# Group 0's low halves all on VectorE, and the first two groups' softmax of q by head on ScalarE

## The chip, the cores and the metric

The kernel runs on one NeuronCore of one Trainium2 chip, as one launch. The metric is the device time of the program in microseconds; lower is better. Three runs of the kernel before took 1586.83, 1587.82 and 1588.03 us; their median is 1587.82 us.

## The reference

A linear attention is followed by two gated feed-forward blocks. q, k and v have the shape (8, 8, 576, 64): batch, heads, positions, features of a head.

```python
q_s = softmax of q over its 64 features      # per position and head
k_s = softmax of k over its 576 positions    # per head and feature
kv  = k_s^T @ v                              # 64 x 64 per head
x   = q_s @ kv, heads side by side           # 4608 tokens x 512
xn  = x / sqrt(mean(x*x) + 1e-6) * rms_g
x   = (silu(xn @ w_gate) * (xn @ w_val)) @ w_out     # d_ff 1536
h   = max(x @ w1, x @ w2, x @ w3)                    # d_ff 768
out = h @ w2_out
```

The softmax of q takes away the maximum of each head first and adds 1e-9 to the sum that it divides by.

## The kernel before

The 4608 tokens are worked on in nine groups of 512 tokens (the ninth collects the last 64 positions of each batch). Each group's attention is made in four pairs of heads, p = 0 to 3; a pair's q is a tile of 128 tokens x 8 x 64 (four blocks of 128 tokens times two heads). While one group runs through the first feed-forward block, the attention of the next is made beside it; group 0's own attention comes first, in a prologue of staged calls (the table `stages`).

**A group's feed-forward** is twelve steps f (`iteration`), one for each 128 of the 1536 inner features. In each, TensorE computes pg (gate) and pv (value), 12 matmuls each, and adds the step before to four accumulators (`out1`), 12 more. Every product is made of three matmuls, on operands that are split in a high part, rounded by ScalarE (ACT), and a low part, the rest of a subtraction: hi*hi, hi*lo and lo*hi. So `hh` and `hl` are the two parts of the hidden values t, `wh` and `wl` those of the weights, `xh` and `xl` those of the input. t itself is tanh on ACT (L651), then two operations on VectorE (DVE): L652, which reads pg, and L663, which reads pv. pg has one bank of PSUM, so pg of a step can start when L652 of the step before has read it.

**The weights come as 64-bit words** and are made into floats on the chip, once, during group 0, one step f + 1 ahead of its use (class `Weights`). A step's weights are two halves h of 128 x 768. For each half, ACT scales the upper words (L144), DVE joins the words in three operations (L149, L150, L151, "the joins" below), ACT rounds the high part (L162) and a subtraction gives the low part (L168): half 0's on GpSimd (POOL), half 1's on DVE. The columns of pg lie in half 0. In group 0 up to step 10 the subtraction for `hl` (L670) is POOL's too, and in all other groups DVE's.

**The softmax of q** (`q_exp`, `q_divide`) takes for a pair: the maximum of each head on DVE (L281, qm), a subtraction on POOL (L282), exp on ACT in place (L283), the sum on DVE (L287, qs), an addition and a reciprocal on DVE (L288, L290) and the product on POOL (L291). After that TensorE transposes q (`transpose_q`). POOL also makes the low part of group 0's input (L389) and adds up squares (L379).

**Group 0's normalisation** is needed only at the first hidden value: pg and pv of steps 0 and 1 are made from the input that is not yet normalised (`raws`), and the result is multiplied by the scale z (L649, giving u_0, and L662). z comes from four sums (var, L410) by a chain of ten small operations on DVE (`token_rstd`, L421 to L426), a transpose on TensorE and a copy on ACT (`spread_rstd`).

A scheduler orders the instructions of each engine when the program is built, by its own estimate of each duration; each engine then works strictly in that order and waits at the first instruction whose inputs are not there. So a line that moves to another engine also moves other instructions. COMPACT is the set of groups 0 and 1, whose scale is computed in the small form.

Of the kernel before, what the change touches and what calls it, by code (L numbers as in the profile page):

```python
# [8 lines left out]
F32 = mybir.dt.float32  # L9
F32R = mybir.dt.float32r  # L10
I32 = mybir.dt.int32
AF = mybir.ActivationFunctionType
ALU = mybir.AluOpType
AX = mybir.AxisListType

P = 128
# [9 lines left out]
COMPACT = (0, 1)  # L26
# [18 lines left out]
def attention_moe_moe(ctx: ExitStack, tc: tile.TileContext, q, k, kt, v, w1, rms_g, w2, w2_out, out):  # L45
# [14 lines left out]
    nc = tc.nc  # L60
# [4 lines left out]
    two = ctx.enter_context(tc.tile_pool(name="two", bufs=2))  # L65
# [3 lines left out]
    def bank(tag, name):  # L69
        return ps.tile([P, N], F32, tag=tag, name=name)  # L70
# [39 lines left out]
    for i in range(2):  # L110
        t = one.tile([P, P], F32, tag=f"kv_raw{i}", name=f"kv_raw{i}")
# [6 lines left out]
    class Weights:  # L118
# [45 lines left out]
        def low(self, f, h):  # L164

            hi = wh[1, f].rearrange("p j n -> p (j n)")[:, h * HALF : (h + 1) * HALF]
            engine = nc.gpsimd if h == 0 else nc.vector
            engine.tensor_sub(self.half(1, f, h), self.y.pop((f, h)), hi.bitcast(F32))  # L168

    class Ahead:  # L170

# [82 lines left out]
    q_t, k_t, kT_t, v_t, kv8 = {}, {}, {}, {}, {}  # L254
    kmax, xraw, sacc, qrt, rstd = {}, {}, {}, {}, {}

    def load_pair(g, p):
# [14 lines left out]
        else:  # L272
            kv8[p] = []
            for i in range(2):
                t = two.tile([P, 4, P], F32, tag=("k", "v")[i], name=f"kv8_{p}_{i}")
                nc.sync.dma_start(t, kv_dram[p, :, 4 * i : 4 * i + 4, :])
                kv8[p].append(t)

    def q_exp(g, p):
        qm = two.tile([P, 24], F32, tag="qm", name=f"qm_{g}_{p}")[:, 0:8]  # L280
        nc.vector.tensor_reduce(qm, q_t[g, p], axis=AX.X, op=ALU.max)  # L281
        nc.gpsimd.tensor_sub(q_t[g, p], q_t[g, p], qm.unsqueeze(2).to_broadcast([P, 8, 64]))  # L282
        nc.scalar.activation(q_t[g, p], q_t[g, p], AF.Exp)  # L283

    def q_divide(g, p):
        qs = two.tile([P, 8], F32, tag="qs", name=f"qs_{g}_{p}")
        nc.vector.tensor_reduce(qs, q_t[g, p], axis=AX.X, op=ALU.add)  # L287
        nc.vector.tensor_scalar(qs, qs, EPS_SM, None, op0=ALU.add)  # L288
        qr = two.tile([P, 8], F32, tag="qr", name=f"qr_{g}_{p}")
        nc.vector.reciprocal(qr, qs)  # L290
        nc.gpsimd.tensor_mul(q_t[g, p], q_t[g, p], qr.unsqueeze(2).to_broadcast([P, 8, 64]))  # L291

    def k_max(g, p):
        if g == NB:
            return
        km = two.tile([P, 1], F32, tag="km", name=f"km_{g}_{p}")
        nc.vector.tensor_reduce(km, kT_t[g, p], axis=AX.X, op=ALU.max)
        kmax[g, p] = km

    def k_exp(g, p):  # L300
        if g == NB:
            return
        pb = pair_bank(g, p, "pb", "a1")
        nc.tensor.transpose(pb[:, 0:P], kmax[g, p].to_broadcast([P, P]), ident)
        nc.vector.tensor_sub(k_t[g, p], k_t[g, p], pb[:, 0:P].unsqueeze(1).to_broadcast([P, 5, P]))
        nc.scalar.activation(k_t[g, p], k_t[g, p], AF.Exp)
# [25 lines left out]
    def transpose_q(g, p):  # L332
        pt = pair_bank(g, p, "pt", "a1")
        for t in range(4):
            nc.tensor.transpose(
                pt[:, t * P : (t + 1) * P], q_t[g, p][:, 2 * t : 2 * t + 2, :].rearrange("p a d -> p (a d)"), ident
            )
        if g in WHOLE:
            if g == 0 and p > 0:
                if p == 1:  # L340
                    sqs["q"] = wpool.tile([P, 3, N], F32, tag="wl5", name="qrts")
                qrt[g, p] = sqs["q"][:, p - 1, :]
            else:
                qrt[g, p] = pair_tile(one, [P, N], F32, "qh", g, p)
            nc.scalar.copy(qrt[g, p], pt)
            return
        qh[g, p] = pair_tile(one, [P, N], F32R, "qh", g, p)
        ql[g, p] = pair_tile(one, [P, N], F32R, "ql", g, p)
        split(qh[g, p], ql[g, p], pt)
# [163 lines left out]
    acc, hh, hl = {}, {}, {}  # L513
# [90 lines left out]
    def iteration(g, nxt, f):  # L604
        ahead = g == 0 and f + 1 < NF1
        pair, odd = f // 2, f % 2

        if ahead:
            first.scale(f + 1, 0)
        if nxt is not None:  # L610
            if not odd and 1 <= pair <= 4:
                transpose_q(nxt, pair - 1)
                make_kv(nxt, pair - 1)
                if pair + 1 < 4:
                    load_pair(nxt, pair + 1)
            if odd and 1 <= pair <= 4:
                make_x(nxt, pair - 1)
            if pair < 4 and not odd:
                k_max(nxt, pair)
                q_exp(nxt, pair)  # L620
            if pair < 4 and odd:
                k_exp(nxt, pair)
                q_divide(nxt, pair)
            if f == 10 and nxt in COMPACT:
                token_rstd(nxt)
            elif f == 10:
                variance(nxt)
                newton_step(nxt, 0)
                newton_step(nxt, 1)
            if f == 11:  # L630
                if nxt not in COMPACT:
                    newton_step(nxt, 2)
                for p in range(4):
                    normalise(nxt, p)
        elif f == 1:
            load_raw(0)
        if ahead:
            first.join(f + 1, 0)
            first.scale(f + 1, 1)
        wkey = (1, f)  # L640
        raw = g == 0 and f < NRAW
        xhs = [(rawh[p] if raw else xh[g, p]) for p in range(4)]
        xls = [(rawl[p] if raw else xl[g, p]) for p in range(4)]
        pg = bank("G", f"pg_{g}_{f}")
        product_in(pg, wh[wkey], wl[wkey], 0, xhs, xls)
        t = two.tile([P, N], F32, tag="t", name=f"t_{g}_{f}")
        if raw:
            u = two.tile([P, N], F32, tag="y", name=f"u_{g}_{f}", bufs=3)
            nc.vector.tensor_mul(u, pg, rstd[0][1])  # L649
            pg = u  # L650
        nc.scalar.activation(t, pg, AF.Tanh, scale=0.5)  # L651
        nc.vector.scalar_tensor_tensor(t, t, 1.0, pg, op0=ALU.add, op1=ALU.mult)  # L652
        if ahead:
            first.high(f + 1, 0)
            first.join(f + 1, 1)
        pv = bank("V", f"pv_{g}_{f}")
        product_in(pv, wh[wkey], wl[wkey], 1, xhs, xls)
        if nxt is not None and f == 11:
            for p in range(4):
                split_x(nxt, p)  # L660
        if raw:
            nc.vector.tensor_mul(t, t, rstd[0][1])  # L662
        nc.vector.tensor_mul(t, t, pv)  # L663
        hh[g, f] = two.tile([P, N], F32R, tag="hh", name=f"hh_{g}_{f}")
        hl[g, f] = two.tile([P, N], F32R, tag="hl", name=f"hl_{g}_{f}")
        nc.scalar.copy(hh[g, f], t)  # L666
        if ahead:
            first.low(f + 1, 0)
            first.high(f + 1, 1)
        (nc.gpsimd if ahead else nc.vector).tensor_sub(hl[g, f], t, hh[g, f].bitcast(F32))  # L670
        if nxt is not None and f == 9 and nxt not in COMPACT:
            split_squares(nxt)
        if f > 0:
            out1(g, f - 1)
        elif g > 0:
            out1(g - 1, NF1 - 1)
        if nxt in COMPACT and f == 10:
            spread_rstd(nxt)
        if g > 0 and nxt is not None:
            if g == 1 and f == 0:  # L680
                second.load()
                second.load()
            second.advance(f)
            if g == NG - 2 and f == NF1 - 1:
                assert not second.steps
        if nxt is None:
            if 1 <= f <= 3:
                fetch(2)
            if f in (4, 5):
                for n in range(4 * f - 16, 4 * f - 12):  # L690
                    combine(0, n)
            if f >= 6:
                for which in {6: (B11,), 7: (T2,), 8: (T1,), 9: (T3,), 10: (B21, B22), 11: (T4,)}[f]:
                    split_operand(which)
            if f == 11:
                fetch_out(0)
        if ahead:
            first.low(f + 1, 1)
            first.load(f + 4)
        if g == 0 and f == NRAW - 1:  # L700
            for p in range(4):
                normalise(0, p)
                split_x(0, p)
# [100 lines left out]
    for pr in range(NPAIR):  # L804
        g = 2 * pr
        for u in range(UNITS):
            fp, j = divmod(u, 3)
            if j == 0:
                t = {
                    key: two.tile([P, N], F32, tag=tag, name=f"t2_{pr}_{fp}_{tag}")  # L810
                    for key, tag in (((0, 0), "q"), ((0, 1), "k"), ((1, 0), "v"), ((1, 1), "t"))
                }
# [23 lines left out]
    g = NG - 1  # L836
    for u in range(UNITS):
        fp, j = divmod(u, 3)
        pair = [bank(tag, f"p2_{g}_{u}_{tag}") for tag in (("G", "V"), ("a0", "a1"))[u % 2]]
        if j == 0:  # L840
            t = [two.tile([P, N], F32, tag=tag, name=f"t2_{g}_{fp}_{tag}") for tag in ("q", "k")]
# [76 lines left out]
```

## Time and profile before

| | |
|---|---|
| median of three runs | 1587.82 us |
| the profiled execution: its own time, and its span | 1587.12 us, 1585.3 us |
| PE busy | 1538.8 us (97% of the span) |
| DVE busy | 865.9 us (55%) |
| ACT busy | 529.3 us (33%) |
| POOL busy | 270.1 us (17%) |
| mean granted TensorE clock | 0.989 |

The span is what the rows lie in; about 1.8 us of the execution lie around it. The shares are means over stages of different kinds. In the page's picture of 40 slices of 40 us, PE is below nine tenths only in the first four, and DVE, which works at five or six tenths later on, is at nine tenths in the first three; POOL has three to five tenths there and two or less afterwards. A row of a timeline is start, duration, engine, line, operation, tiles and shape. A duration on DVE is the time from an instruction's start to its end, and it contains time in which the instruction could not get on.

### The profile page before, as it was taken

The page shows a single profiled execution, that of the slowest core. Times are in us where ns is not written, and L with a number is a line of the kernel's source. Part 1 is how long each engine was busy: PE and PEld are TensorE (multiplying, and loading weights), DVE is VectorE, ACT ScalarE, POOL GpSimd, SP SyncE. Part 2 cuts the span into 40 slices and gives each one's busy share as a digit, 9 for nine tenths or more (in the row PEclk, how much of TensorE's full clock was granted, in tenths as well). Part 3 has the DMA queues.
Part 4 walks back from the last instruction along what each step waited for, and adds up shares of the span by engine and source line. Part 5 has one row for each costly group of instructions (what it writes and reads, how often), then busy time and mean ns, then how long its engine had stood idle before and what let it go on. Part 6 is the DMA issues. An engine that isn't in the chain of part 4 may idle for free.

```text
span 1585.3 us, 18644 instructions
## 1 busy us (share of the span) xinstructions
PE 1538.8 (97%) x6974; PEld 1269.1 (80%) x6974; DVE 865.9 (55%) x1450; ACT 529.3 (33%) x919; POOL 270.1 (17%) x308
## 2 busy tenths in 40 slices
PE   5788999999999999999999999999999999999999
PEld 3566788888888888888888888888888888888887
DVE  6999654655655655656552243535645644634412
ACT  4553433433433444344332231322322322322221
POOL 4355222122120231221200100001001001001000
PEclk8899999999999999999999999999999999999999
DMA  7662143331340541434301013164544554444441
GB/s 258 238 226 84 61 138 106 104 119 53 126 133 24 164 139 62 152 115 139 100 22 53 14 47 127 53 226 163 187 175 164 183 177 164 161 173 165 134 153 47
DMA packets 92889, 203.33 MB, mean 128 GB/s; under 512 B 8448, under 2 KB 36096, under 8 KB 92800
## 3 DMA queue, kind: packets, MB, share of 16 engines
q1 hardware_dynamic: 82432, 183.27, 34.6%
q10 hardware_dynamic: 10368, 18.88, 3.2%
q8 instruction: 55, 0.90, 0.2%
q14 instruction: 34, 0.28, 0.1%
HBM read 161.48 MB, written 40.63 MB: 127 GB/s over the span
## 4 chain that ended last, share of the span: by engine, by line
PE 90%; DVE 5%; DMA 1%; issue 1%; POOL 1%; ACT 0%; SPq 0%; DVEq 0%; POOLq 0%; ACTq 0%
PE acc L482 9%; PE acc L481 9%; PE acc L483 9%; PE pg L475 6%; PE pg L477 6%; PE pg L476 6%; PE pv L477 6%; PE pv L476 6%; PE pv L475 6%; PE p_a L481 5%; PE p_a L483 5%; PE p_a L482 5%; PE p_G L481 2%; PE p_G L483 2%; PE p_G L482 2%; PE pk L315 2%
## 5 line engine op out<-in xcount | busy, mean ns | idle before, releaser
L652 DVE SCALAR_TENSOR_TENSOR t<-t,pg 128x512 f32<-128x512 f32 x106 | 72.7, 686 | 129.2 <-ACT t L651 127.6
L775 POOL TENSOR_TENSOR temps_wl<-temps_wh 128x512 f32<-128x512 f32 x36 | 46.5, 1292 | 525.8 <-ACT temps_wh L774 517.5
L666 ACT CAST hh<-t 128x512 fp32r<-128x512 f32 x108 | 66.9, 619 | 158.8 <-DVE t L663 158.4
L663 DVE TENSOR_TENSOR t<-t,pv 128x512 f32<-128x512 f32 x108 | 73.3, 679 | 62.0 <-PE pv L477 61.0
L651 ACT ACTIVATE t<-pg 128x512 f32<-128x512 f32 x106 | 62.9, 594 | 126.4 <-PE pg L477 126.3
L670 DVE TENSOR_TENSOR hl<-t,hh 128x512 fp32r<-128x512 f32 x97 | 70.4, 725 | 57.4 <-ACT hh L666 56.6
L483 PE MATMUL p_a<-x_wh,chunk 128*128 128x512 f32 x240 | 93.4, 389 | 0.0
L481 PE MATMUL p_a<-x_wh,chunk 128*128 128x512 f32 x240 | 93.4, 389 | 0.0
L482 PE MATMUL p_a<-x_wl,chunk 128*128 128x512 f32 x236 | 91.8, 389 | 0.0
L772 DVE TENSOR_TENSOR temps_wh<-temps_wh,p_V 128x512 f32<-128x512 f32 x36 | 24.7, 685 | 116.1 <-PE p_V L483 116.1
L482 PE MATMUL acc<-wo_lo,h 128*128 128x512 f32 x216 | 84.8, 392 | 0.0
L481 PE MATMUL acc<-wo_hi,h 128*128 128x512 f32 x216 | 84.6, 392 | 0.0
L483 PE MATMUL acc<-wo_hi,l 128*128 128x512 f32 x216 | 84.4, 391 | 0.0
L227 POOL TENSOR_TENSOR wq<-st,wq 128x256 fp32r<-128x256 f32 x63 | 47.5, 770 | 166.2 <-ACT wq L226 160.3
L282 POOL TENSOR_TENSOR q<-q,qm 128x512 f32<-128x512 f32 x34 | 39.3, 1155 | 163.6 <-DVE qm L281 153.4
L770 ACT COPY temps_wh<-p_G 128x512 f32<-128x512 f32 x36 | 21.1, 586 | 136.6 <-PE p_G L483 136.3
L483 PEld LDWEIGHTS p_a<-x_wh,chunk 128*128 128x128 f32 x240 | 45.1, 188 | 9.4
L481 PEld LDWEIGHTS p_a<-x_wh,chunk 128*128 128x128 f32 x240 | 45.0, 188 | 9.3
L482 PEld LDWEIGHTS p_a<-x_wl,chunk 128*128 128x128 f32 x236 | 44.3, 188 | 9.2
L291 POOL TENSOR_TENSOR q<-q,qr 128x512 f32<-128x512 f32 x34 | 38.7, 1138 | 63.5 <-DVE qr L290 63.5
L481 PEld LDWEIGHTS acc<-wo_hi,h 128*128 128x128 f32 x216 | 40.6, 188 | 9.2
L481 PE MATMUL p_G<-x_wh,chunk 128*128 128x512 f32 x123 | 47.8, 389 | 0.0
(481 smaller groups left out, 4291.2 us busy)
## 6 DMA issues: line engine op xcount, KB each, us to landing
chunk<-w_dram SPq DMA_DIRECT2D x84, 768.0 KB, 4.2
words<-in_w SPq DMA_DIRECT2D x24, 768.0 KB, 7.2
w_dram<-wq SPq DMA_DIRECT2D x63, 256.0 KB, 2.3
k<-in_k SPq DMA_DIRECT2D x30, 320.0 KB, 3.6
v<-in_v SPq DMA_DIRECT2D x30, 320.0 KB, 4.4
st<-in_w SPq DMA_DIRECT2D x18, 512.0 KB, 4.2
x<-xe ACTq DMA_DIRECT2D x36, 256.0 KB, 2.4
out<-oe ACTq DMA_DIRECT2D x36, 256.0 KB, 2.0
```

What stands on the lines that cost most here:

```text
L227: nc.gpsimd.tensor_sub(t[:, 1, :], src, t[:, 0, :].bitcast(F32))
L475: nc.tensor.matmul(pt, hi[:, j, s], xhs[kk], start=(kk == 0), stop=False)
L476: nc.tensor.matmul(pt, hi[:, j, s], xls[kk], start=False, stop=False)
L477: nc.tensor.matmul(pt, lo[:, j, s], xhs[kk], start=False, stop=(kk == 3))
L481: nc.tensor.matmul(pt, ah, bh, start=first, stop=False, skip_group_check=onto)
L482: nc.tensor.matmul(pt, ah, bl, start=False, stop=False, skip_group_check=onto)
L483: nc.tensor.matmul(pt, al, bh, start=False, stop=last, skip_group_check=onto)
L651: nc.scalar.activation(t, pg, AF.Tanh, scale=0.5)
L652: nc.vector.scalar_tensor_tensor(t, t, 1.0, pg, op0=ALU.add, op1=ALU.mult)
L663: nc.vector.tensor_mul(t, t, pv)
L666: nc.scalar.copy(hh[g, f], t)
L670: (nc.gpsimd if ahead else nc.vector).tensor_sub(hl[g, f], t, hh[g, f].bitcast(F32))
```

## The change

Three edits. `low` takes DVE for both halves, so the twelve subtractions of half 0 leave POOL. The subtraction for `hl` in group 0 (eleven of them) is DVE's as everywhere else. In groups 0 and 1 `q_exp` no longer subtracts on POOL: DVE negates the eight maxima of a row, and ACT takes exp head by head, eight instructions of 128 x 64, each with the negated maximum as its bias and with the sum of its results written beside it (`accum_out`). `q_divide` then needs no sum on DVE. The later groups keep the old form.

```diff
--- before.py
+++ after.py
@@ -164,8 +164,7 @@
         def low(self, f, h):
 
             hi = wh[1, f].rearrange("p j n -> p (j n)")[:, h * HALF : (h + 1) * HALF]
-            engine = nc.gpsimd if h == 0 else nc.vector
-            engine.tensor_sub(self.half(1, f, h), self.y.pop((f, h)), hi.bitcast(F32))
+            nc.vector.tensor_sub(self.half(1, f, h), self.y.pop((f, h)), hi.bitcast(F32))
 
     class Ahead:
 
@@ -276,15 +275,28 @@
                 nc.sync.dma_start(t, kv_dram[p, :, 4 * i : 4 * i + 4, :])
                 kv8[p].append(t)
 
+    qsum = {}
+
     def q_exp(g, p):
         qm = two.tile([P, 24], F32, tag="qm", name=f"qm_{g}_{p}")[:, 0:8]
         nc.vector.tensor_reduce(qm, q_t[g, p], axis=AX.X, op=ALU.max)
+        if g in COMPACT:
+            qs = two.tile([P, 8], F32, tag="qs", name=f"qs_{g}_{p}")
+            qsum[g, p] = qs
+            nc.vector.tensor_scalar(qm, qm, -1.0, None, op0=ALU.mult)
+            for i in range(8):
+                head = q_t[g, p][:, i, :]
+                nc.scalar.activation(head, head, AF.Exp, bias=qm[:, i : i + 1], accum_out=qs[:, i : i + 1])
+            return
         nc.gpsimd.tensor_sub(q_t[g, p], q_t[g, p], qm.unsqueeze(2).to_broadcast([P, 8, 64]))
         nc.scalar.activation(q_t[g, p], q_t[g, p], AF.Exp)
 
     def q_divide(g, p):
-        qs = two.tile([P, 8], F32, tag="qs", name=f"qs_{g}_{p}")
-        nc.vector.tensor_reduce(qs, q_t[g, p], axis=AX.X, op=ALU.add)
+        if g in COMPACT:
+            qs = qsum.pop((g, p))
+        else:
+            qs = two.tile([P, 8], F32, tag="qs", name=f"qs_{g}_{p}")
+            nc.vector.tensor_reduce(qs, q_t[g, p], axis=AX.X, op=ALU.add)
         nc.vector.tensor_scalar(qs, qs, EPS_SM, None, op0=ALU.add)
         qr = two.tile([P, 8], F32, tag="qr", name=f"qr_{g}_{p}")
         nc.vector.reciprocal(qr, qs)
@@ -667,7 +679,7 @@
         if ahead:
             first.low(f + 1, 0)
             first.high(f + 1, 1)
-        (nc.gpsimd if ahead else nc.vector).tensor_sub(hl[g, f], t, hh[g, f].bitcast(F32))
+        nc.vector.tensor_sub(hl[g, f], t, hh[g, f].bitcast(F32))
         if nxt is not None and f == 9 and nxt not in COMPACT:
             split_squares(nxt)
         if f > 0:
```

The order of the instructions changes with it, up to the first steps of group 1; from there on the instructions of PE, DVE, ACT and SP stand in the order that they had.

On DVE at the end of the prologue, between the sums of squares (var) and u_0, there stands before (z0 and a0 are the small chain's tiles, y_2 the weights of step 2, wl_(1, 1) the low part of step 1):

```order
L421 TENSOR_SCALAR z0_0_369<-var0_0_364 128x4
L149 TENSOR_SCALAR y_2_493<-y_2_493 128x768
L424 SCALAR_TENSOR_TENSOR a0_0_371<-z0_0_369 128x4
L150 SCALAR_TENSOR_TENSOR y_2_493<-words_2_0_413,y_2_493 128x768
L425 TENSOR_TENSOR a0_0_371<-a0_0_371,var0_0_364 128x4
L168 TENSOR_TENSOR wl_(1, 1)_484<-y_1_431,wh_(1, 1)_461 128x768
L426 SCALAR_TENSOR_TENSOR z0_0_369<-a0_0_371,z0_0_369 128x4
L151 SCALAR_TENSOR_TENSOR y_2_493<-words_2_0_413,y_2_493 128x768
```

and after the change:

```order
L422 TENSOR_SCALAR var0_0_388<-pv_0_3_356 128x1
L433 TENSOR_SCALAR z0_0_393<-var0_0_388 128x4
L436 SCALAR_TENSOR_TENSOR a0_0_395<-z0_0_393 128x4
L437 TENSOR_TENSOR a0_0_395<-a0_0_395,var0_0_388 128x4
L438 SCALAR_TENSOR_TENSOR z0_0_393<-a0_0_395,z0_0_393 128x4
...
L302 RECIPROCAL qr_1_0_532<-qs_1_0_461 128x8
L167 TENSOR_TENSOR wl_(1, 1)_516<-y_1_455,wh_(1, 1)_493 128x768 x2
L661 TENSOR_TENSOR u_0_0_489<-pg_0_0_475,z_0_410 128x512
L317 TENSOR_TENSOR k_1_0_431<-k_1_0_431,pb_1_0_527 128x640
```

The joins of step 2 have left the chain of small operations: y_2 is now joined behind u_0. Both halves' low parts of step 1 stand directly ahead of u_0.

On DVE around step 5 of group 0 (t_0_5) there stands before (words_7 and y_7 are the weights of step 7, wl_(1, 6) the low part of step 6):

```order
L168 TENSOR_TENSOR wl_(1, 6)_939<-y_6_878,wh_(1, 6)_917 128x768
L150 SCALAR_TENSOR_TENSOR y_7_960<-words_7_0_773,y_7_960 128x768
L652 SCALAR_TENSOR_TENSOR t_0_5_914<-t_0_5_914,pg_0_5_901 128x512
L151 SCALAR_TENSOR_TENSOR y_7_960<-words_7_0_773,y_7_960 128x768
L149 TENSOR_SCALAR y_7_960<-y_7_960 128x768
L663 TENSOR_TENSOR t_0_5_914<-t_0_5_914,pv_0_5_922 128x512
L150 SCALAR_TENSOR_TENSOR y_7_960<-words_7_1_775,y_7_960 128x768
L287 TENSOR_REDUCE qs_1_3_1064<-q_1_3_801 128x8
L151 SCALAR_TENSOR_TENSOR y_7_960<-words_7_1_775,y_7_960 128x768
```

and after the change:

```order
L151 SCALAR_TENSOR_TENSOR y_6_922<-words_6_0_730,y_6_922 128x768
L664 SCALAR_TENSOR_TENSOR t_0_5_956<-t_0_5_956,pg_0_5_943 128x512
L150 SCALAR_TENSOR_TENSOR y_6_922<-words_6_1_732,y_6_922 128x768
L675 TENSOR_TENSOR t_0_5_956<-t_0_5_956,pv_0_5_964 128x512
L151 SCALAR_TENSOR_TENSOR y_6_922<-words_6_1_732,y_6_922 128x768
L682 TENSOR_TENSOR hl_0_5_979<-t_0_5_956,hh_0_5_978 128x512
L167 TENSOR_TENSOR wl_(1, 6)_981<-y_6_922,wh_(1, 6)_959 128x768 x2
```

The joins beside step 5 are now those of step 6 and no longer those of step 7, and hl of the step and both low halves of step 6 stand behind L675, the new number of L663 (L664 is the old L652).

On ACT at the start of the program (q_0_0 is the first pair's q, k_0_0 its k, the tiles wh8, wl8 and wh10 hold q and k of the third and fourth pair) there stands before:

```order
L283 ACTIVATE q_0_0_120<-q_0_0_120 128x512
L306 ACTIVATE k_0_0_122<-k_0_0_122 128x640
L283 ACTIVATE q_0_1_130<-q_0_1_130 128x512
L306 ACTIVATE k_0_1_132<-k_0_1_132 128x640
L283 ACTIVATE wh8_0_2_140<-wh8_0_2_140 128x512
L306 ACTIVATE wl8_0_2_142<-wl8_0_2_142 128x640
L345 COPY qh_0_0_257<-pt_0_0_252 128x512
```

and after the change:

```order
L289 ACTIVATE q_0_0_120,qs_0_0_170<-q_0_0_120,qm_0_0_168 128x64 x8
L289 ACTIVATE q_0_1_130,qs_0_1_188<-q_0_1_130,qm_0_1_186 128x64 x2
L318 ACTIVATE k_0_0_122<-k_0_0_122 128x640
L289 ACTIVATE q_0_1_130,qs_0_1_188<-q_0_1_130,qm_0_1_186 128x64 x6
L318 ACTIVATE k_0_1_132<-k_0_1_132 128x640
L289 ACTIVATE wh8_0_2_140,qs_0_2_206<-wh8_0_2_140,qm_0_2_204 128x64 x8
L318 ACTIVATE wl8_0_2_142<-wl8_0_2_142 128x640
L289 ACTIVATE wh10_0_3_150,qs_0_3_228<-wh10_0_3_150,qm_0_3_226 128x64 x8
```

Each exp of a pair's q is now eight instructions on ACT, and the first copy of a transposed q (qh) comes behind the fourth pair's k.

## Rows read from the trace of the kernel before

**Rows 1.** Busy time by stretch: us, PE, PEld, DVE, ACT, POOL, clock, DMA, GB/s.
```profile
80.00:100.00 20.00, 19.45 (x92) 15.61 (x90) 20.00 (x24) 11.43 (x17) 10.34 (x8) 1.00 0.66 252
200.00:220.00 20.00, 20.00 (x98) 16.69 (x97) 12.76 (x27) 8.19 (x16) 5.41 (x8) 1.00 0.57 191
```

**Rows 2.** Waits of PE, 58 to 182 us: total us, times, longest.
```profile
PE pg L475 <- DVE t L652: 8.9, 6, 2.8
```

**Rows 3.** Timeline of PE, first matmul of pg_3, pg_4, pg_10: start, us.
```profile
81.30 0.48 PE L475 MATMUL pg<-xh,wh_(1, 3)_653 128*128 128x512 f32 x1
...
91.03 0.48 PE L475 MATMUL pg<-xh,wh_(1, 4)_734 128*128 128x512 f32 x1
...
166.10 0.79 PE L475 MATMUL pg<-xh,wh_(1, 10)_1245 128*128 128x512 f32 x1 [2.19 <-DVE t L652]
```

**Rows 4.** Timeline of DVE, a stretch in which POOL idles.
```profile
126.58 1.03 DVE L149 TENSOR_SCALAR y<-y 128x768 int32<-128x768 int32 x2
...
128.25 1.82 DVE L150 SCALAR_TENSOR_TENSOR y<-words,y 128x768 int32<-128x768 int32 x2
...
130.58 1.82 DVE L151 SCALAR_TENSOR_TENSOR y<-words,y 128x768 int32<-128x768 int32 x2
132.32 1.65 DVE L149 TENSOR_SCALAR y<-y 128x768 int32<-128x768 int32 x1
```

**Rows 5.** Timelines of DVE (two rows) and POOL (two), 110 to 115 us.
```profile
110.48 2.58 DVE L168 TENSOR_TENSOR wl_(1, 6)_939<-y,wh_(1, 6)_917 128x768 fp32r<-128x768 f32 x1
112.98 2.01 DVE L150 SCALAR_TENSOR_TENSOR y<-words,y 128x768 int32<-128x768 int32 x1
...
110.10 2.13 POOL L168 TENSOR_TENSOR wl_(1, 6)_939<-y,wh_(1, 6)_917 128x768 fp32r<-128x768 f32 x1
112.19 1.98 POOL L379 TENSOR_TENSOR sacc<-sacc,sq 128x512 f32<-128x512 f32 x1
```

**Rows 6.** DVE by line and shape, 57 to 165 us: busy us, mean ns.
```profile
L150 DVE SCALAR_TENSOR_TENSOR y<-words,y 128x768 int32<-128x768 int32 x18 | 21.6, 1209 | 0.0
L151 DVE SCALAR_TENSOR_TENSOR y<-words,y 128x768 int32<-128x768 int32 x18 | 18.6, 1040 | 0.0
L149 DVE TENSOR_SCALAR y<-y 128x768 int32<-128x768 int32 x18 | 15.4, 863 | 0.1
L663 DVE TENSOR_TENSOR t<-t,pv 128x512 f32<-128x512 f32 x9 | 6.1, 675 | 0.0
```

**Rows 7.** Line 168 alone, 57 to 165 us: DVE busy, POOL busy.
```profile
57.00:165.00 108.00, 16.20 (x10) 18.07 (x10) 0.94 0.41 140
```

**Rows 8.** By line and shape, 230 to 1100 us: DVE, then POOL.
```profile
L670 DVE TENSOR_TENSOR hl<-t,hh 128x512 fp32r<-128x512 f32 x92 | 66.9, 727 | 54.8 <-ACT hh L666 54.1
...
L291 POOL TENSOR_TENSOR q<-q,qr 128x512 f32<-128x512 f32 x24 | 25.1, 1047 | 50.7 <-DVE qr L290 50.7
```

**Rows 9.** Timeline of DVE, 44 to 59 us, up to u_0.
```profile
44.10 0.83 DVE L410 TENSOR_SCALAR var<-pv 128x1 f32<-128x1 f32 x4 [0.30 <-PE pv L396]
...
49.04 0.94 DVE L168 TENSOR_TENSOR wl_(1, 1)_484<-y,wh_(1, 1)_461 128x768 fp32r<-128x768 f32 x1
...
58.72 0.68 DVE L649 TENSOR_TENSOR u<-pg,z 128x512 f32<-128x512 f32 x1
```

**Rows 10.** Timeline of ACT: the first weight step and the third xraw.
```profile
24.72 0.93 ACT L144 ACTIVATE y<-words 128x768 f32<-128x768 f32 x1
...
38.63 0.69 ACT L368 ACTIVATE xraw<-px,gain 128x512 f32<-128x512 f32 x1 [5.94 <-PE px L358]
```

**Rows 11.** The chain in order of time, 22 to 60 us: start, us.
```profile
31.90 1.99 POOL wl_(1, 0)_400 L168
...
33.95 0.79 PE pv L477
```

**Rows 12.** ACT by line and shape: whole span, then 0 to 176 us.
```profile
L89 ACT CAST kvh<-kv_raw 128x128 fp32r<-128x128 f32 x24 | 7.1, 298 | 30.5 <-DVE kv_raw L325 30.3
...
L283 ACT ACTIVATE q<-q 128x512 f32<-128x512 f32 x8 | 5.0, 631 | 13.0 <-POOL q L282 12.9
```

## The prediction

> **What bounds the kernel now.** I read the busy time by stretch first. Early in group 1 TensorE works all 20.00 of 20 us and DVE 12.76; between 80 and 100 us DVE has 20.00 of 20 and POOL 10.34 [rows 1]. So the program has two parts: from group 1 on TensorE sets the time, and what moves there is worth little; in group 0 DVE works without a break. The waits of TensorE in group 0 say the same: 8.9 us in six waits of pg for DVE's L652 [rows 2], which has to read the bank before pg can be written again. The pace of the steps is in the timeline of TensorE: pg_3 to pg_4 takes 9.73 us, TensorE's own pace, but pg_3 to pg_10 takes 84.80 us for seven steps, 12.1 each [rows 3]. About 2.4 us a step are lost to DVE.
>
> Then I asked whether DVE's time is work. Where POOL idles, two L149 and one L652 take 1.67 us from start to next start, two L150 and an L663 2.33, two L151 1.74: 0.50, 0.87 and 0.87 us an operation and 0.6 for the t's [rows 4]. Beside POOL the same operations are longer: a DVE L168 takes 2.58 us and ends at 113.06, just after POOL's L168 (110.10 to 112.23); the L150 behind it takes 2.01 and ends at 114.99, after POOL's L379 (112.19 to 114.17) [rows 5]. Alone, L168 takes 0.94 [rows 9] and L150 0.91 [rows 4]. L663, which reads PSUM, keeps its 675 ns [rows 6]. Between 57 and 165 us the means are 1209, 1040 and 863 ns for L150, L151 and L149, 18 each [rows 6]; against busy times of 0.91, 0.91 and 0.52 [rows 4] that is 5.4, 2.3 and 6.2 us too long. Ten DVE L168 took 16.20 us [rows 7] where 9.4 would do: 6.8. Together 20.7 us in 108, nearly nine steps: 2.3 us a step in which DVE stands beside POOL. The Trainium skill (SBUF — State Buffer, "SBUF: two separate sides") calls this a lock: a DVE instruction with two SBUF inputs or in a two-port mode and a GpSimd instruction exclude each other for a whole instruction. The trace agrees, down to the ends of the rows quoted; by that rule each product and sum left on POOL goes on blocking too, which I allow for below from rows.
>
> **What the change does, part by part.**
>
> *Lows and hl.* POOL loses 12 L168 and 11 L670 and with L282 the subtraction of the softmax. DVE gains per step a low half, 0.87 as an L150 of the same length, and hl, about 0.65 (0.727 busy in later groups [rows 8], some 0.07 of it overlapped): 1.5 us. It loses a sum L287 every second step (about 0.6) and gets a negation on eight columns, less than 0.2: 0.2 us a step less. Left on POOL in two steps are one L291 of 1.05 us [rows 8] and one L379, where some nine us stood before, so I keep a quarter of the stretch, 0.6. The order also has DVE join one step's weights per step, where before it ran up to a step and a half ahead and did 47 joins in seven steps instead of 42 (5 by 0.75, 0.5 a step), and three reductions for group 2 leave the stretch (0.25 a step). 12.1 − 2.3 + 0.6 + 1.5 − 0.2 − 0.5 − 0.25 = 10.95; from the pitches directly it is six joins 4.5, two lows 1.7, two t's 1.2, hl 0.65, 1.5 for the attention of group 1, 0.6 for POOL: 10.2. I take 10.5. Eight steps from pg_3 to pg_11 gain 8 × 1.6 = 12.8. The start costs some of it: the joins of step 2, before u_0 until now, come behind it, 4.5 us, and nothing hides them, since pg_3 then waits for its low half. Gain −8. Bounds: with a step of 9.73, TensorE's own, −14; with the stretch kept where POOL is left and a wait for ACT's hh in every step (hl now holds the low half queued behind it on DVE, and that holds pg), 11.5 a step and about 0.
>
> *The prologue up to u_0.* Two things go. First, ACT idles 5.94 us before the third xraw [rows 10]; the chain shows POOL's low half of step 0 from 31.90 for 1.99 us, late behind two raws in POOL's row, then TensorE's pv that needs it [rows 11], and px behind it on TensorE, which works in order. Now both halves follow DVE's own joins at 0.87. I count −6 with the head start that the first joins get (ACT's first weight step, 24.72 [rows 10], is now put ahead of the first xraw). Second, var starts at 44.10 and u_0 at 58.72 [rows 9], 14.6 us for fourteen operations on a few columns and a short transpose and copy, because joins, a low half and reductions stand between them on DVE. Afterwards they stand together: at 0.2 each (var's four took 0.83) 3 us, and 3 for transpose and copy: −8. Against this stands ACT: eight exps instead of one of 631 ns [rows 12]. No row has a 64-wide one with a bias and a sum. A 128-wide cast takes 298 ns [rows 12], about 0.2 in pitch; a piece can't cost more than the whole, about 0.55. So 1.6 to 4.4 us a pair; I take 3, nearer the short row, with room for the sum. Four pairs add 9.5 us to ACT before the first copy of q, most of it where ACT waited for POOL's subtraction and the loads: 2 us shown. Sum −12. Bounds: −15 with short pieces, −4 with pieces of 0.55. The Trainium skill (ScalarE: Activation LUTs, "What ACT_TABLE_LOAD costs") gives 280 ns + 0.833 ns a column with a bias from a tile and an overlap of 93, an estimate of 240 ns a piece; its fixed part speaks against cutting one exp in eight. By it a pair would be 1.9 us and the time about 1 us better; no row here shows it.
>
> *Group 1.* The order moves reductions and the first joins of the second block's weights out of group 0, some 7 us of DVE work. DVE has 7 of 20 us free there [rows 1], so I count +1.5, between 0 and +5. Behind that the order is the old one, and what group 0 gains stays gained because TensorE is behind nothing else.
>
> Sum: −12 − 8 + 1.5 = −18.5. The profiled execution's own 1587.12 us becomes 1568.6; the median lies 0.7 above it, so 1569 us.
>
> **Rivals.** *TensorE becomes the bound in group 0.* All waits go, steps run at 9.73, and u_0 comes 15 us earlier: −14 − 15 + 1.5, about 1560. For it: six waits of one kind make up what TensorE loses. Against it: my step on DVE is above 9.73 even from clean pitches. *The prologue keeps its length.* Pieces of exp near 0.55 delay k, the transposes and the first joins, so that the early start is spent: −2 − 8 + 1.5, about 1579. For it: ACT is in order, and k's exps stand between the pieces. *An even trade:* blocking on the little that POOL keeps falls on the worst places, and pg waits on ACT each step: 1587. *DVE is the bound and only gets more work.* If the stretch of L149 to L168 does not come from POOL but from anything that stays (TensorE's reads, the loads), DVE pays 12 × 0.87 + 11 × 0.65 less eight sums, about 15 us, and gets nothing: 1602. It decides as soon as less than three quarters of the 20.7 us go away and the prologue gives nothing. Against it: the ends that fall together in rows 5, and that L663 is never stretched.
>
> **How the numbers follow.** Forecast 0.55 (1560 to 1579 by its own bounds, midst 1569), TensorE bound 0.15, prologue kept 0.2, even trade 0.05, slower 0.05. The range is 1558 to 1582: it holds the first three with the edges of their bounds and leaves out the last two and some tail. About 0.2% (3 us) is what a measurement tells from no change. Faster 0.9, same 0.05, slower 0.05.
>
> **What would show it.** In the profile after: u_0 near 47 us instead of 58.72; pg_3 to pg_10 in about 74 us; L150 and L149 near 0.95 and 0.55 on the mean in group 0; POOL below 3 of 20 us there; the pieces of exp at 0.2 to 0.55 us. Wrong would be: joins as long as before with POOL empty, pieces above 0.5, or TensorE waiting for DVE's low half or ACT's hh for more than 1 us in each step.

## The result and the profile after

The changed kernel takes 1563.97 us (median of five runs, 1561.35 to 1568.54) against 1587.82: the ratio is 0.9859, 95% interval 0.9838 to 0.9880. The execution that was profiled took 1568.5 us (span 1566.7). One reading of the page of before has to be put right: DVE is at nine tenths in the second to fourth slice of 40 us, not in the first three (the first has six), and POOL has its three to five tenths in the first four.

Busy time by stretch, of the kernel after; the columns are those of [rows 1]:

```profile
80.00:100.00 20.00, 19.28 (x89) 14.88 (x88) 19.92 (x33) 13.61 (x32) 1.76 (x3) 1.00 0.81 301
...
140.00:160.00 20.00, 20.00 (x94) 16.09 (x93) 19.94 (x38) 11.45 (x17) 2.99 (x2) 1.00 0.05 15
200.00:220.00 20.00, 20.00 (x97) 16.75 (x96) 11.00 (x22) 6.42 (x11) 3.60 (x5) 1.00 0.22 65
```

POOL falls from 10.34 to 1.76 of 20 us, and DVE is as full as before, but it gets through 33 instructions where it had 24. By line and shape on DVE, 57 to 150 us (busy us, mean ns):

```profile
L151 DVE SCALAR_TENSOR_TENSOR y<-words,y 128x768 int32<-128x768 int32 x18 | 17.3, 963 | 0.0
L150 DVE SCALAR_TENSOR_TENSOR y<-words,y 128x768 int32<-128x768 int32 x17 | 16.2, 951 | 0.0
L149 DVE TENSOR_SCALAR y<-y 128x768 int32<-128x768 int32 x17 | 12.3, 729 | 0.1
L675 DVE TENSOR_TENSOR t<-t,pv 128x512 f32<-128x512 f32 x10 | 6.8, 678 | 0.0
```

Against [rows 6], the mean of L150 fell by 258 ns, that of L149 by 134 and that of L151 by 77, and that of L675, which is L663 of before and reads PSUM, stayed. The pace, in TensorE's timeline (the first matmuls of pg_3, pg_10 and pg_11):

```profile
79.39 0.50 PE L487 MATMUL pg<-xh,wh_(1, 3)_691 128*128 128x512 f32 x1 [3.05 <-ACT wh_(1, 3)_691 L162]
...
149.41 0.49 PE L487 MATMUL pg<-xh,wh_(1, 10)_1293 128*128 128x512 f32 x1
...
157.72 0.39 PE L487 MATMUL pg<-xh,wh_(1, 11)_1374 128*128 128x512 f32 x1
```

Before, pg_11 stood at

```profile
176.90 0.48 PE L475 MATMUL pg<-xh,wh_(1, 11)_1326 128*128 128x512 f32 x1
```

pg_3 to pg_10 takes 70.02 us, 10.0 a step, where [rows 3] had 12.1. The waits of TensorE (30 to 182 us: total us, times, longest) no longer name t, as [rows 2] did; the longest, and the longest behind pg_3, are

```profile
PE pg L487 <- ACT wh_(1, 3)_691 L162: 3.0, 1, 3.0
...
PE pg L489 <- DVE wl_(1, 8)_1160 L167: 0.9, 1, 0.9
```

The end of the prologue on DVE, against [rows 9] (var to u_0 14.62 us there, 5.47 here):

```profile
47.83 0.83 DVE L422 TENSOR_SCALAR var<-pv 128x1 f32<-128x1 f32 x4 [1.50 <-PE pv L408]
48.70 0.17 DVE L433 TENSOR_SCALAR z<-var 128x4 int32<-128x4 int32 x1
...
50.48 0.16 DVE L438 SCALAR_TENSOR_TENSOR z<-a,z 128x4 f32<-128x4 f32 x1
...
53.30 0.68 DVE L661 TENSOR_TENSOR u<-pg,z 128x512 f32<-128x512 f32 x1
```

and the third xraw on ACT, against [rows 10], with the first of the pieces of exp behind it:

```profile
41.22 0.69 ACT L380 ACTIVATE xraw<-px,gain 128x512 f32<-128x512 f32 x1 [4.50 <-PE px L370]
...
42.79 0.36 ACT L289 ACTIVATE q<-q,qm 128x64 f32<-128x64 f32 x1
43.04 0.20 ACT L289 ACTIVATION_READ_ACCUMULATOR q<-q,qm 128x1 f32 x1
43.13 0.34 ACT L289 ACTIVATE q<-q,qm 128x64 f32<-128x64 f32 x1
```

So the steps gained more than was foreseen, and the prologue, in this execution, less: var is 3.7 us later than before.

### The profile page after: what moved, and what is told of

Read it like the earlier page. It is cut to its first block, busy times and chain, and to the rows that moved or that the text cites. A ratio compares the mean times of both kernels' runs of the same rounds, so it can differ in the third digit from the quotient of the medians.

```text
span 1566.7 us, 18735 instructions
## 1 busy us (share of the span) xinstructions
PE 1538.4 (98%) x6974; PEld 1269.4 (81%) x6974; DVE 854.7 (55%) x1473; ACT 547.2 (35%) x1039; POOL 219.7 (14%) x277
## 4 chain that ended last, share of the span: by engine, by line
PE 93%; DVE 4%; DMA 1%; issue 1%; ACT 0%; SPq 0%; DVEq 0%
PE acc L494 9%; PE acc L493 9%; PE acc L495 9%; PE pg L487 6%; PE pg L489 6%; PE pg L488 6%; PE pv L487 6%; PE pv L488 6%; PE pv L489 6%; PE p_a L493 5%; PE p_a L495 5%; PE p_a L494 5%; PE p_G L493 2%; PE p_G L495 2%; PE p_G L494 2%; PE pk L327 2%
## 5 line engine op out<-in xcount | busy, mean ns | idle before, releaser
L664 DVE SCALAR_TENSOR_TENSOR t<-t,pg 128x512 f32<-128x512 f32 x106 | 72.8, 687 | 126.5 <-ACT t L663 124.8
L663 ACT ACTIVATE t<-pg 128x512 f32<-128x512 f32 x106 | 63.2, 596 | 134.5 <-PE pg L489 134.0
L682 DVE TENSOR_TENSOR hl<-t,hh 128x512 fp32r<-128x512 f32 x108 | 78.7, 729 | 56.9 <-ACT hh L678 56.1
L675 DVE TENSOR_TENSOR t<-t,pv 128x512 f32<-128x512 f32 x108 | 73.5, 680 | 59.9 <-PE pv L489 58.6
L291 POOL TENSOR_TENSOR q<-q,qm 128x512 f32<-128x512 f32 x28 | 31.0, 1108 | 144.3 <-DVE qm L282 144.2
L391 POOL TENSOR_TENSOR sacc<-sacc,sq 128x512 f32<-128x512 f32 x24 | 32.1, 1336 | 120.8 <-ACT sq L390 117.1
```

What stands on the lines that cost most here:

```text
L682: nc.vector.tensor_sub(hl[g, f], t, hh[g, f].bitcast(F32))
```

## Experiments: which edit pays

Theory: POOL's subtractions kept DVE waiting, so the lows and hl bring the gain. Rival: the softmax does, through the prologue. Five kernels take back a part of the change each; a sixth (e0_again) is the changed kernel itself, to see its spread. Edits are against the changed kernel.

*e1_low_hl*: `if g in COMPACT:` becomes `if False:` in `q_exp` and `q_divide`. *e3_exp_g1*: it becomes `if g == 1:`. *e2_exp* takes back the other part:

```diff
-            nc.vector.tensor_sub(self.half(1, f, h), ...)
+            engine = nc.gpsimd if h == 0 else nc.vector
+            engine.tensor_sub(self.half(1, f, h), ...)
-        nc.vector.tensor_sub(hl[g, f], t, ...)
+        (nc.gpsimd if ahead else nc.vector).tensor_sub(hl[g, f], t, ...)
```

*x_lows* takes back only the second of these two (hl on POOL), *x_hl* only the first (low half 0 on POOL).

> The changed kernel once more, unaltered, to see what its five runs of 1561 to 1569 us vary with, and as the base of the others. Theory A (the prologue's matmuls run at one of the two levels of TensorE's clock, and which is chance): another profile shows u_0 between 45 and 53 us and a total that follows it one for one; median 1561 to 1568. Theory B (the variation lies in group 0's steps or later): u_0 stays at 53 within 1 us and the steps differ.

> Lows and hl on DVE, the softmax of q as before on POOL, ACT and DVE. Theory A (what counts is that POOL's large subtractions no longer hold DVE up): most of the gain stays, steps pg_3 to pg_10 at 10.0 to 10.6 us each, L150 at 1.0 to 1.05 us, total 1565 to 1573. Theory B (the softmax edit is what frees the prologue and POOL): steps above 11.3 us, total 1577 to 1585.

> The softmax edit alone; the low halves of half 0 and group 0's hl stay on POOL. Theory A: POOL still holds DVE up, L150 at 1.1 us or more and steps above 11.3 us, total 1578 to 1587. Theory B: total 1565 to 1575.

> As the change, but the softmax edit only for group 1; group 0's prologue has the old softmax (subtraction on POOL, one exp, sum on DVE). Theory A (64 pieces of exp and their reads of the sum on ACT are what kept the prologue from getting shorter than 53.3 us to u_0): u_0 at 46 to 50 us, total 1557 to 1561. Theory B (ACT had room; TensorE's own slow stretch and the order set the prologue): u_0 at 52 to 56 us, total 1563 to 1568.

> The changed kernel with hl of group 0 back on POOL: only the lows are on DVE. By the lock that the subtractions on POOL showed, what counts is POOL's two-input time in the steps: hl leaves 1.6 to 1.7 us a step of it, where the changed kernel has about 1.3 us a step of other POOL work and the kernel before some 5. The steps should come to 10.4 to 10.8 us instead of 10.0 (12.1 before) and the time to 1567 to 1571 us. Rival: hl on POOL is worse than its length, since TensorE's acc and the bank of pg wait for it behind ACT's hh; then steps of 11 us or more and 1574 us or later.

> The changed kernel with the first low half of each step back on POOL: only hl is on DVE. A low half is 1.8 to 2.1 us of POOL's two-input time a step, so steps near 10.5 to 11 us, L150 and L151 near 1.0 to 1.05 us, time 1568 to 1573 us. Rival: the low half on POOL costs no more than hl there, or nothing, because DVE is spared a low half of 0.87 us a step; then 10.0 to 10.2 us a step and 1562 to 1566 us.

Median, ratio to the kernel before with its interval, and from each profile u_0, pg_3 and us a step from pg_3 to pg_10:

| kernel | on DVE | softmax | median us | ratio | u_0 | pg_3 | a step |
|---|---|---|---|---|---|---|---|
| before | | old | 1587.82 | 1 | 58.72 | 81.30 | 12.1 |
| after | lows, hl | new | 1563.97 | 0.9859 (0.9838 to 0.9880) | 53.30 | 79.39 | 10.0 |
| e0_again | lows, hl | new | 1566.08 | 0.9856 (0.9836 to 0.9876) | 46.76 | 71.58 | 10.0 |
| e1_low_hl | lows, hl | old | 1564.73 | 0.9854 (0.9839 to 0.9868) | 53.79 | 75.39 | 9.9 |
| e3_exp_g1 | lows, hl | new in group 1 | 1564.56 | 0.9851 (0.9835 to 0.9868) | 51.12 | 76.24 | 9.9 |
| e2_exp | | new | 1585.59 | 0.9991 (0.9982 to 1.0000) | 49.52 | 75.30 | 11.9 |
| x_lows | lows | new | 1574.60 | 0.9922 (0.9909 to 0.9936) | 50.33 | 76.69 | 10.4 |
| x_hl | hl | new | 1586.10 | 0.9984 (0.9974 to 0.9993) | 51.80 | 85.26 | 10.5 |

The lows and hl together have the whole gain (e1); the softmax alone has next to none. e3, which was to tell whether the pieces of exp hold the prologue up, has a u_0 (51.12) between those of its two theories and the time of the second. e2 shows why the softmax alone gives so little: its u_0 comes 9.2 us earlier than before and its pg_3 6.0, but its steps keep their 11.9 us. Where group 0 ends, TensorE waits 4.0 us for the scale of group 1, whose chain on DVE the order now puts among joins, and of the lead 1.9 us are left at group 1's pg_1 (191.50 against 193.38).

The parts don't add up: lows alone save about 14 us, hl alone 2.5, both 23. My expectation for x_hl failed by 13 us, and for x_lows by 4. In both the steps up to pg_10 came as expected (10.4 and 10.5); the rest lies outside them. In x_lows it is mostly a wait of 4.7 us for group 1's scale, as in e2. x_hl's profiled run is 18.3 us longer than that of the changed kernel: pg_3 comes 5.9 us later, the seven steps take 3.7 more, and pg_10 to pg_11 takes 16.0 us instead of 8.3, with a wait of 2.0 us for POOL's low half of step 10, one of 3.4 for group 1's scale, and matmuls of 0.63 us behind each of them where 0.39 is the rule. The waits for the scale come with the order on DVE, so these kernels do not price the two subtractions apart. x_hl's first loss comes from one low half on POOL. POOL's timeline:

```profile
64.82 6.24 POOL L168 TENSOR_TENSOR wl_(1, 2)_580<-y,wh_(1, 2)_557 128x768 fp32r<-128x768 f32 x1
85.28 1.83 POOL L168 TENSOR_TENSOR wl_(1, 3)_713<-y,wh_(1, 3)_691 128x768 fp32r<-128x768 f32 x1 [14.23 <-ACT wh_(1, 3)_691 L162]
```

and DVE's beside the first of them:

```profile
64.81 0.68 DVE L90 TENSOR_TENSOR xl<-xraw,xh 128x512 fp32r<-128x512 f32 x1
65.41 0.68 DVE L473 TENSOR_TENSOR xraw<-xraw,z 128x512 f32<-128x512 f32 x1
...
68.09 1.28 DVE L473 TENSOR_TENSOR xraw<-xraw,z 128x512 f32<-128x512 f32 x2
69.29 0.15 DVE L332 TENSOR_SCALAR ks<-pk 128x1 f32<-128x1 f32 x1
69.36 0.67 DVE L283 TENSOR_REDUCE qm<-q 128x8 f32<-128x512 f32 x1
69.95 1.65 DVE L90 TENSOR_TENSOR xl<-xraw,xh 128x512 fp32r<-128x512 f32 x1
```

The same subtraction takes 6.24 us instead of 1.83. It ends at 71.06; 1.83 before that is 69.23, just when DVE's run of instructions with two SBUF inputs (64.81 to 69.3) gives way to a small one that reads PSUM. So POOL seems to have stood for 4.4 us behind DVE; then DVE's L90 at 69.95, which otherwise takes 0.68, ended at 71.60, 0.54 after POOL. TensorE paid for it: it waits 5.1 us for wl_(1, 2).

## Experiments: is it POOL's work as such

The kernels above also move DVE's own work and the order. These two leave that work where it is: they give POOL work that no one waits for, beside the changed kernel's steps. Both have the same order on DVE, ACT and TensorE; against the changed kernel it differs in a few places.

```diff
         nc.scalar.copy(hh[g, f], t)
+        if ahead and f >= 2:
+            nc.scalar.copy(extra[:, 0:1], t[:, 0:1])
+            for _ in range(4):    # x_sub: 128 x 384, two inputs in SBUF
+                nc.gpsimd.tensor_sub(extra, ident (three times), ones_f (three times))
+            for _ in range(12):   # x_set instead: the same 128 x 384, no input
+                nc.gpsimd.memset(extra, 1.0)
```

> The changed kernel with work put back on POOL that no one waits for: in the steps of group 0 from the third on, four subtractions of 128x384 from two constant SBUF tiles into a tile that nothing reads, let go by an ACT copy of one column of t; DVE's, ACT's and TensorE's orders are otherwise nearly as before. Theory A (a POOL instruction with two SBUF inputs keeps DVE's products waiting for its whole length): POOL gets about 4.5 us a step (a 512-wide one took 1.57 to 1.69 us), DVE's L150, L151 and L149 rise from 0.95 to 1.00, 0.96 and 0.70 to 0.72 us to about 1.15, 1.03 and 0.85, and a step goes from 10.0 towards 11.5 to 12; time 1574 to 1580 us. Theory B (the steps gained because hl and the lows are made earlier or in another order, and POOL's activity as such costs nothing): means and steps stay, 1560 to 1568 us.

> The same kernel with twelve memsets of 128x384 in place of the four subtractions of each step: about the same POOL time, but nothing is read from SBUF. Theory A in the narrow form (only POOL instructions that read SBUF hold up a DVE instruction with two SBUF inputs): L150 and L151 keep about 1.0 and 0.96 us, at most L149, which has one input, is stretched (0.72 to 0.85), steps 10.0 to 10.5, time 1562 to 1569 us. Theory A in the broad form (any POOL instruction blocks): as with the subtractions, 1574 to 1580 us. Theory B: 1560 to 1568 us.

x_sub took 1590.94 us (ratio 1.0022, 1.0013 to 1.0032), x_set 1569.63 (0.9885, 0.9870 to 0.9899). pg_3 and pg_10 stand at 73.94 and 164.97 us in x_sub, at 79.40 and 151.48 in x_set. A stretch of x_sub (busy time), and behind it by line and shape POOL and DVE, 75 to 160 us:

```profile
100.00:120.00 20.00, 16.77 (x67) 12.38 (x66) 19.25 (x25) 7.39 (x13) 14.62 (x12) 0.85 0.26 79
```

```profile
L684 POOL TENSOR_TENSOR extra<-ident,ones_f 128x384 bf16<-128x384 f32 x28 | 40.8, 1456 | 52.6 <-ACT extra L682 51.0
...
L168 DVE TENSOR_TENSOR wl_(1, 7)_1106<-y,wh_(1, 7)_1079 128x768 fp32r<-128x768 f32 x2 | 3.5, 1768 | 0.0
```

The same stretch and lines of x_set:

```profile
100.00:120.00 20.00, 18.59 (x86) 14.35 (x86) 19.85 (x32) 11.62 (x33) 13.23 (x28) 1.00 0.36 107
```

```profile
L684 POOL MEMSET extra<- 128x384 bf16 x96 | 43.5, 453 | 46.0 <-ACT extra L682 41.5
...
L168 DVE TENSOR_TENSOR wl_(1, 7)_1146<-y,wh_(1, 7)_1111 128x768 fp32r<-128x768 f32 x2 | 1.8, 952 | 0.0
```

POOL's time is about the same (40.8 and 43.5 us). With the subtractions a low half on DVE takes 1768 ns and a step 13.0 us; with the memsets 952 ns and 10.3 us. POOL instructions that read two SBUF tiles and that nobody needs take back the whole gain of the change; as many microseconds of writing take back some 4 us of it. Part of x_sub's loss may be TensorE's clock, which is 0.85 in its stretch and 1.00 in that of x_set. That settles the theory in its narrow form for POOL's subtractions against its memsets (a POOL instruction that reads one tile was not tried); my 1574 to 1580 us for x_sub was too mild. This comes as the Trainium skill (SBUF — State Buffer, "SBUF: two separate sides") has it, which limits the block on a DVE instruction with two SBUF inputs to GpSimd instructions that read SBUF; x_hl shows that it holds in both directions.

Writing is not free either. L149, which has one input, is lengthened by the memsets alone (x_set, where it is L150, on DVE, and POOL beside it):

```profile
94.55 1.65 DVE L150 TENSOR_SCALAR y<-y 128x768 int32<-128x768 int32 x2
...
91.74 4.81 POOL L684 MEMSET extra<- 128x384 bf16 x9
```

Two of them take 1.65 us where [rows 4] has 1.03. The two-input joins that are long in x_set, four between 75 and 160 us, all lie beside a product or subtraction that POOL has in the changed kernel too.

## Experiments: the prologue and the spread

The changed kernel's own runs go from 1560.42 to 1568.54 us. Its second profiled run (e0_again) took 1560.42, the first 1568.5; of the 8.1 us between them 7.8 are there at pg_3 already (71.58 and 79.39). The timeline of TensorE in the profile after, matmuls of group 0's attention:

```profile
20.97 2.49 PE L327 MATMUL pk<-wh,wl 128*128 128x129 f32 x10 [1.81 <-DVE gain L511]
...
28.35 2.06 PE L370 MATMUL px<-qrts,kv_raw 128*128 128x512 f32 x2
...
37.46 2.35 PE L327 MATMUL pk<-wh,wh 128*128 128x129 f32 x10
39.60 1.58 PE L370 MATMUL px<-qrts,kv_raw 128*128 128x512 f32 x2
```

and in e0_again, the same program:

```profile
20.02 2.49 PE L327 MATMUL pk<-wh,wl 128*128 128x129 f32 x10 [1.92 <-DVE gain L511]
...
26.72 1.10 PE L370 MATMUL px<-qrts,kv_raw 128*128 128x512 f32 x2
...
33.37 1.38 PE L327 MATMUL pk<-wh,wh 128*128 128x129 f32 x10 [0.29 <-DVE kv_raw L337]
34.59 1.02 PE L370 MATMUL px<-qrts,kv_raw 128*128 128x512 f32 x2
```

The same matmuls take 2.06 and 2.35 us in one and 1.10 and 1.38 in the other, about the two to one of the levels 1.2 and 2.4 GHz. The clock column doesn't show all of it: between 20 and 25 us it is 0.50 for e0_again, but 1.00 for the profile after, where the same long durations stand. The profile of x_set has the durations of the profile after and pg_3 at 79.40 us, and there the column says 0.50:

```profile
25.00:40.00 15.00, 13.50 (x47) 10.49 (x46) 9.14 (x13) 8.78 (x14) 3.30 (x5) 0.50 0.34 121
```

f1_fill and f2_fill_less test the cause: matmuls whose result is overwritten keep TensorE busier in the prologue.

```diff
+    def keep_warm(tile, n):
+        for _ in range(n):
+            nc.tensor.matmul(tile, ones, ones (four times), start=True, stop=True)
         pk = pair_bank(g, p, "pk", "a0")
+        if g == 0:
+            keep_warm(pk, (0, 4, 5, 2)[p])   # px: 0, 1, 1, 0; pt: 0, 3, 2, 2; pv_0: 3
```

f2_fill_less has (0, 0, 0, 1), (0, 0, 1, 0), (0, 0, 1, 2) and 2, and five in a free bank. b1_chain is e1_low_hl with all of DVE's work for steps 1 and 2, but the joins of step 1, tied behind the end of the chain (`tc.issue_after`); w1_chain_fill is that with 40 such matmuls.

> The lows and hl on DVE with the old softmax, and in the prologue everything that DVE does for steps 1 and 2, except the joins of step 1, queued behind the chain from var to z. Theory A (the chain's neighbours, not the softmax, decide when u_0 comes, and half of what u_0 gains is kept, since DVE has the same work before step 3): var to u_0 5 to 6 us instead of 11.9, u_0 near 47.5 instead of 53.8, pg_3 near 72 instead of 75.4, steps 9.9; time 1560 to 1562 us. Theory B (DVE is full from 45 to 65 us, so its order there changes nothing): u_0 early, but pg_3 stays near 75 and the time at 1564 to 1565 us.

> The kernel before in this list, and in the prologue 40 matmuls of 512 columns whose result is overwritten, put into banks before their real use, so that TensorE stands still less there. Theory A (the prologue's length hangs on the pace of TensorE, which fell to the 1.2 GHz level in parts of it: ten pk in 2.5 us instead of 1.35, a 512-wide matmul each 0.43 us instead of 0.22): pk, px and pv keep the short durations from about 20 us on, u_0 and pg_3 come 1 to 3 us earlier, and the time is 1557 to 1561 us with a small spread. Theory B (the extra matmuls stand in the way, or the prologue waits for loads and ACT anyway): u_0 no earlier, 1561 to 1565 us.

> The changed kernel with 24 matmuls of 512 columns in the prologue whose result is overwritten, put into the banks of pk, px, pt and pv before their real use. Theory A (the spread of the changed kernel from 1560 to 1568 us is the pace of TensorE in the prologue, at the 1.2 GHz level from 20 to 48 us in its slow runs): the durations of pk, px and pv are the short ones from about 24 us on in the profiled run, var near 42 instead of 47.8, and all runs lie within 2 us at 1560 to 1562 us. Theory B (the spread has another cause, the loads for one): the spread stays, 1560 to 1568 us, or the extra matmuls delay the prologue and all runs lie at 1564 us or later.

> The changed kernel with 12 such matmuls instead of 24, none of them ahead of pk_1 and px_1, and four in a bank of their own behind pk_1, where TensorE stood still for 1.92 us in the fast run of the changed kernel. In the kernel with 24, var came at 43.36 against 41.19 in that run, because the ones ahead of pk_1 and pk_2 ran at the 1.2 GHz level and put each of them off by some 2 us. Theory A (the pace stays up with 12 and nothing is put off): pk and px short from about 24 us on, var at 41 to 42 us, all runs within 2 us at 1559.5 to 1561.5 us, below the kernel with 24. Theory B (12 are too few to hold the pace in every run): runs spread from 1560 to 1568 us again.

| kernel | runs, us | median | ratio | var | u_0 | pg_3 |
|---|---|---|---|---|---|---|
| f1_fill | 1561.84 to 1564.06 | 1562.43 | 0.9843 (0.9829 to 0.9856) | 43.36 | 49.20 | 74.02 |
| f2_fill_less | 1562.41 to 1566.78 | 1563.06 | 0.9853 (0.9836 to 0.9869) | 41.56 | 47.59 | 73.64 |
| b1_chain | 1565.26 to 1568.68 | 1567.79 | 0.9868 (0.9854 to 0.9883) | 43.55 | 48.40 | 76.25 |
| w1_chain_fill | 1566.66 to 1567.30 | 1567.06 | 0.9866 (0.9851 to 0.9881) | 43.96 | 48.81 | 76.66 |

That is 23 matmuls in f1_fill (its expectation counts 24). In its timeline the last pair is short where it was long in the profile after:

```profile
35.66 1.28 PE L334 MATMUL pk<-wh,wh 128*128 128x129 f32 x10
36.77 1.02 PE L381 MATMUL px<-qrts,kv_raw 128*128 128x512 f32 x2
```

and its runs lie within 2.2 us instead of 8.1; w1's within 0.6 instead of b1's 3.4. The mean clocks on record point the same way in e0_again (0.998 in the run of 1560.42 us, 0.991 to 0.994 in the other three) and in f2 (0.995 in the run of 1566.78, 0.998 to 0.999 in the others), but not in the first five runs, where the two longest have 0.998 and two shorter ones 0.994. Against the matmuls stands that e1 and e3 have no such matmuls and yet lie within 1.2 and 1.0 us. So it is well supported that the pace sets the two profiles apart; that the matmuls narrow the spread is not shown by four or five runs a kernel. With twelve of them one run of f2 still took 1566.78. f1_fill has the lowest median of all and beats the kernel before clearly; against the changed kernel it is 1.5 us lower, but the intervals overlap, and it lies just above the 1560 to 1562 us expected. w1_chain_fill missed its first theory: its u_0 and pg_3 come no earlier than b1's, and its time is the same.

b1_chain went against its first theory. Counted from var, its u_0 came 7.0 us before e1's (4.85 against 11.90), its pg_3 only 0.8 (32.70 against 33.50), and its steps, 10.3 us, took the rest back: it is 3 us slower than e1. In e1 DVE works 10.00 of the 10 us from 45 to 55, so the joins for step 2 that made room for the chain came late (the last starts at 61.34 us instead of 52.33), and so did what stands behind them: b1's pg_3 waits 3.0 us for the high part of its weights, e1's for nothing. f2 repeats that on a small scale: var 1.8 us before f1's, pg_3 only 0.4.

## Why the prediction was right

| stretch | forecast | before | after | e0_again |
|---|---|---|---|---|
| start to u_0 | −12 | 58.72 | 53.30: −5.4 | 46.76: −12.0 |
| u_0 to pg_3 | +4.5 | 22.58 | 26.09: +3.5 | 24.82: +2.2 |
| pg_3 to pg_11 | −12.8 | 95.60 | 78.33: −17.3 | 78.00: −17.6 |
| pg_11 to the end | +1.5 | 1410.22 | 1410.78: +0.6 | 1410.84: +0.6 |
| sum (time of the profiled run) | −18.5 | 1587.12 | 1568.50: −18.6 | 1560.42: −26.7 |

(The terms add up to −18.8; the sum took −12.8 + 4.5 as −8.) The sum agrees with the first profile only because its terms missed in opposite directions: that is luck. The median, 1563.97, is 5 us below the forecast of 1569 and inside the range.

*Lows and hl.* The mechanism is shown (x_sub, x_set). The size was too small: a step takes 9.8 us (78.33 over eight), not 10.5. The forecast also took 12.1 for all eight steps before, while the eighth took 10.80; by its own 10.5 the term is −11.6. Both of my sums kept 0.6 us a step of lengthening for what POOL still does. What is left on the joins and lows is some 0.35 (an estimate): between 57 and 150 us four of 17 L149 and one of 18 L151 are long, 3.3 us too long together, all beside a product, a sum or a subtraction on POOL; the others take 0.55 and 0.95. One of the four on DVE, and POOL beside it:

```profile
84.79 1.40 DVE L149 TENSOR_SCALAR y<-y 128x768 int32<-128x768 int32 x1
...
84.22 1.55 POOL L303 TENSOR_TENSOR q<-q,qr 128x512 f32<-128x512 f32 x1 [23.71 <-DVE qr L302]
```

With 0.35 in place of 0.6 the sum from clean pitches is 9.9, near what was measured; the other, 10.7, stays too long, and where is open. L150 and L151 came as forecast (951 and 963 ns on the mean), L149, forecast at 0.55, has 0.73 because of those four, and POOL, forecast below 3 of 20 us, has up to 3.7. TensorE's clock had no term at all. The eight steps before and after, in the columns of [rows 1]:

```profile
81.30:176.90 95.60, 82.26 (x352) 63.94 (x351) 91.51 (x128) 41.52 (x62) 46.42 (x33) 0.95 0.38 130
79.39:157.72 78.33, 75.92 (x347) 60.20 (x348) 77.88 (x128) 44.60 (x89) 12.19 (x13) 1.00 0.42 145
```

Of the 17.3 us, 10.9 are idle time of TensorE (13.3 before, 2.4 after) and 6.3 are its busy time, at a mean clock of 0.95 before and 1.00 after. How much of that second part lay on the path that set the pace no run shows. Now both engines are full: half of the rival in which TensorE becomes the bound came true, and 9.73 us is not its floor (pg_9 to pg_10 takes 9.44). That pg would wait for ACT's hh in every step did not come: the waits between 80 and 182 us are below 1 us each.

*The chain to u_0.* 14.6 us became 5.5 (forecast 6), and e1, where the joins stay in between, has 11.9. That part was right. What it is worth was not: e1 has the old chain and the same time, and in b1 DVE had to make up the work that stepped aside.

*ACT's idle time before the third xraw.* Forecast −6 with the head start of the joins; in the first profile xraw came 2.6 us later than before (41.22 against 38.63), in e0_again 3.0 earlier (35.65). The row of ACT names TensorE's px, and it was the pace of TensorE, which I had not counted as a term, that lay between the two. Even in e0_again var starts only 2.9 us earlier than before (41.19 against 44.10), where the forecast had 4 (6 less 2 for ACT), and the chain gives 9.1 instead of 8: that their sum is the −12 is luck too.

*The pieces of exp.* They start 0.33 us apart, 2.65 us a pair (forecast 3). A piece is two instructions, as the last fence of the first section shows: 337 ns for the exp, of which 240 to 250 pass until the next starts, and 190 for reading the sum, with 90. The estimate of 240 ns a piece by the Trainium skill (ScalarE: Activation LUTs, "What ACT_TABLE_LOAD costs") agrees for the exp and leaves out the sum.

*The rivals.* The prologue kept its length in neither profile of the changed kernel (u_0 53.30 at the latest). That DVE would only get more work is excluded by x_sub and x_set (its price, about 15 us, is 12.8 by the terms given). The softmax edit, which draws the chain together and so carries 8 us of the forecast, is worth nothing measurable on top of the rest: the medians of e1 and e3 lie within 0.6 us of that of the changed kernel's nine runs, 1565.13.

## What to carry to other kernels

Where DVE is full and its two-input rows are longer beside POOL's, look for POOL instructions with two SBUF inputs, not for POOL's share: here taking some 4 us of them a step away, most of it onto the full engine, made the step 2 us shorter. Taking away the low halves alone gave 14 of the 23 us, hl alone 2.5. An early first value that a full engine pays for with its other work was worth next to nothing here (b1, and the softmax edit on top of the rest); ask what steps aside for it. Look at two profiles of the same program before a term of the prologue is read off one.

## What the runs showed of the hardware

- POOL can be held up too: a subtraction of 1.83 us took 6.24 while DVE ran instructions with two SBUF inputs back to back (x_hl).
- POOL memsets leave a DVE low half at 0.95 us but lengthen L149, which has one input: two of them took 1.65 us instead of 1.03 (x_set).
- Reading an accumulated sum on ACT is an instruction of its own (187 to 190 ns, 90 until the next starts, after).
- Matmul durations and the clock column can disagree: ten pk in 2.49 us beside a column at 1.00 (after), and as many in 2.49 beside 0.50 (e0_again).
